# One DMA of 96 partitions for each part of x, a table in parts of 17 and 10 slots, small work on GpSimd, and the first v one step earlier

## The chip, the cores and the metric

The kernel runs on one core of one Trainium2 chip. The metric is the device time of an execution in microseconds.

## The reference

```python
# x: (8, 3072, 256), float32
X = np.fft.fft(np.fft.fft(x, axis=1), axis=2).real      # FNet mixing
x_prev = X shifted by one row along the sequence (zero first)
xk = mu_k * X + (1 - mu_k) * x_prev
xr = mu_r * X + (1 - mu_r) * x_prev
k  = maximum(xk @ w_k, 0)                                # 256 -> 1024
v  = (k * k) @ w_v                                       # 1024 -> 256
out = sigmoid(xr @ w_r) * v                              # (8, 3072, 256), float32
```

## The kernel before

The sequence of 3072 rows is split as 48 x 64. A half of one batch's x lies in a tile `xh` of 96 partitions: partition 48g + n1 holds rows 32g + 16h + (0 to 15) of row block n1. GpSimd issues the loads, which also turn float32 into float16:

```python
x_r = x.rearrange("b (n1 r) d -> b n1 r d", r=R)         # R = 64, N1 = 48, D = 256

def load_part(b, h, n, q0, nq):
    for g in range(2):
        r0 = 32 * g + 16 * h + q0
        nc.gpsimd.dma_start(out=xh_t[b, h][48 * g:48 * g + 48, q0:q0 + nq],
                            in_=x_r[b, :, r0:r0 + nq, :])

def load_xh(b, h):                                       # batches 1 to 7
    xh_t[b, h] = xh_pool.tile([96, 16, 256], FP16, name="xh")    # bufs=2
    load_part(b, h, 1, 0, 16)
```

Per batch, 27 rows of `f` are laid into one partition of `y` by a small DMA, and each pair of finished output tiles is stored by two DMAs of 128 KB from a ring of three buffers. Both are issued by SyncE on one queue, and VectorE waits for them when it reads `y` or reuses `o`:

```python
def flat(b):
    V.memset(y_t[b, "f"][0:1, 0:1], 0.0)
    nc.sync.dma_start(out=y_t[b][0:1, 1], in_=y_t[b, "f"])          # "y<-f"

def v_out(c, tb, n):
    o = o_pool.tile([P, 2, 256], FP32, name="o" ..., bufs=3 if n == 2 else 1)
    V.scalar_tensor_tensor(out=o..., in0=st["v"]..., scalar=16.0, in1=st["r", c]..., ...)
    for s in range(2):
        ...
        eng.dma_start(out=dst, in_=o[64 * s:64 * s + 64, 0:n])      # "out_dram<-o"
```

The rest is one list of 192 steps (one per piece of the k product), to which the other work of this batch and the next is pinned by hand (`v_out` finishes a pair of output tiles); the order on every engine is fixed.

Of the kernel before, what the change touches and what calls it, by code (L numbers as in the profile page):

```python
# [35 lines left out]
def kernel(  # L36
# [18 lines left out]
    NS1 = 9  # L55
# [46 lines left out]
    def load_part(b, h, n, q0, nq):  # L102

        for g in range(2):
            r0 = 32 * g + 16 * h + q0
            nc.gpsimd.dma_start(out=xh_t[b, h][48 * g:48 * g + 48, q0:q0 + nq],  # L106
                                in_=x_r[b, :, r0:r0 + nq, :])

    def load_xh(b, h):
        xh_t[b, h] = xh_pool.tile([96, 16, 256], FP16, name="xh")  # L110
        load_part(b, h, 1, 0, 16)
# [36 lines left out]
    load_part(0, 0, 2, 0, 8)  # L148
# [4 lines left out]
    load_part(0, 0, 2, 8, 8)  # L153
# [5 lines left out]
    load_part(0, 1, 2, 0, 8)  # L159
    load_part(0, 1, 2, 8, 4)  # L160
    load_part(0, 1, 2, 12, 4)
# [136 lines left out]
    def m_rest(part):  # L298



        s = 26 if part else 0
        if part:
            V.tensor_scalar(out=m2[hi64, 25], in0=m1[hi64, 25], scalar1=-1.0, scalar2=None,
                            op0=ALU.mult)
            V.tensor_copy(out=m1[hi64, 25], in_=m1[lo64, 25])
        for n, m in enumerate((m1, m2)):
            V.tensor_scalar(out=m[hi64, s], in0=m[hi64, s], scalar1=-1.0, scalar2=None,
                            op0=ALU.mult)
            if part:  # L310
                V.memset(m[lo64, 25], 0.0)
            else:
                V.tensor_copy(out=mz[lo64, n], in_=m[lo64, 1])
                V.memset(m[:, 0, 0:1], 0.0)
# [11 lines left out]

    g_zeros(13, 24)
# [8 lines left out]
    def loads():  # L336

        V.memset(mu_f, 0.0)
        mus = [mu.rearrange("(a b) -> a b", b=1) for mu in (moe_mu_k, moe_mu_r)]
        for i, mu in enumerate(mus):  # L340
            nc.sync.dma_start(out=mu_f[0:1, 0, i:i + 1], in_=mu[0:1])
            nc.sync.dma_start(out=mu_f[1:65, 0, i:i + 1], in_=mu[1:129:2][0:64])
            nc.sync.dma_start(out=mu_f[65:128, 0, i:i + 1], in_=mu[2:128:2])
        for a in range(2):
            gather(wk_sb[0][a], moe_w_k, a)
        for i, mu in enumerate(mus):
            gather(mu_f[:, 1, i:i + 1], mu, 1)
        load_xh(1, 0)
        for a in range(2):
            gather(wr_sb[0][a], moe_w_r, a)  # L350
        nc.gpsimd.dma_start(out=wv_sb, in_=moe_w_v.rearrange("(fc p) v -> p fc v", p=128))
        load_xh(1, 1)
        for a in range(2):
            gather(wk_sb[1][a], moe_w_k, 2 + a)
        for a in range(2):
            gather(wr_sb[1][a], moe_w_r, 2 + a)
# [12 lines left out]
    def plain_128():  # L369

        V.memset(w_eo[:, 0, 63:64], 1.0)
        V.tensor_scalar(out=w_eo[:, 0, 127:128], in0=w_eo[:, 0, 127:128], scalar1=-2.0,
                        scalar2=1.0, op0=ALU.mult, op1=ALU.add)
        V.memset(u128, 0.0)

        V.tensor_copy(out=tw[lo64, 0, 1:NSL], in_=m1[lo64, 1:NSL, 0])
        V.tensor_copy(out=tw[hi64, 0, 1:NSL], in_=m2[hi64, 1:NSL, 0])
        V.tensor_copy(out=tw[hi64, 1, 1:NSL], in_=m1[hi64, 1:NSL, 0])
        V.tensor_scalar(out=tw[lo64, 1, 1:NSL], in0=m2[lo64, 1:NSL, 0], scalar1=-1.0,
                        scalar2=None, op0=ALU.mult)  # L380
        V.memset(tw[hi64, :, 1:2], 0.0)

        for n, half, sign in ((0, lo64, 1.0), (0, hi64, -1.0), (1, lo64, -1.0), (1, hi64, 1.0)):
            V.tensor_scalar(out=tw[half, n, 0:1], in0=tw[half, n, 2:3], scalar1=sign,
                            scalar2=None, op0=ALU.mult)
# [55 lines left out]
    def d_half(b, u, ps, eng):  # L441
        d_units(b, ps, u, 2)
        evac(g_all[:, u:u + 2, 1:257],
             ps[:, 0:512].rearrange("p (i c) -> p i c", c=256), eng)

# [81 lines left out]
    def mix_short(b, lo, hi):  # L527

        x_t[b, 0, 0] = xo = x_t.get((b, 0, 0)) or mix_pool.tile([P, 2, 1536], FP16, name="x00")
        for a in range(2):  # L530
            V.scalar_tensor_tensor(out=xo[:, a, 64 * lo:64 * hi],
                                   in0=_v(x_t[b], 64 * (26 * a + lo), [(1, 64 * (hi - lo))]),
                                   scalar=mu_f[:, a, 0:1],
                                   in1=_v(y_t[b], 64 * (NSL * a + lo), [(1, 64 * (hi - lo))]),
                                   op0=ALU.mult, op1=ALU.add)
# [4 lines left out]

    def mix2(b, j, m, lo, hi):
        for a in range(2):
            mix(b, j, m, a, lo, hi)
# [41 lines left out]
    def v_tile(c, tb):  # L585

        apart = c == chunks[-1] and tb >= 2
        h = 0 if apart else tb % 2
        if h == 0:
            st["v"] = ps_v()  # L590
        for fc in range(8):
            nc.tensor.matmul(out=st["v"][:, 256 * h:256 * h + 256],  # L592
                             lhsT=k2_t[c][:, fc, 128 * tb:128 * tb + 128],
                             rhs=wv_sb[:, fc], start=(fc == 0), stop=(fc == 7))

    def v_out(c, tb, n):
        b, m, i = c
        o = o_pool.tile([P, 2, 256], FP32, name="o" if n == 2 else f"o{tb}",
                        bufs=3 if n == 2 else 1)
        t0 = tb + 1 - n  # L600

        V.scalar_tensor_tensor(out=o.rearrange("p a b -> p (a b)")[:, 0:256 * n],  # L602
                               in0=st["v"][:, 0:256 * n], scalar=16.0,
                               in1=st["r", c][:, 256 * t0:256 * (t0 + n)],
                               op0=ALU.mult, op1=ALU.mult)
        for s in range(2):
            k = 24 * m + 8 * i + 2 * t0 + s
            dst = dataclasses.replace(out[b, k:k + 1, :], ap=[[48 * D, 64], [2 * D, n], [1, D]])
            eng = nc.scalar if s and n == 1 else nc.sync
            eng.dma_start(out=dst, in_=o[64 * s:64 * s + 64, 0:n])  # L610
# [10 lines left out]
    m_rest(0)  # L621
    loads()
    m_angles(NS1, NSL)
# [8 lines left out]
    m_wrap(NS1, NSL)  # L632
# [7 lines left out]
    d_item(0, 2)  # L640
    m_sine(NS1, NSL)
    d_item(0, 3)
    for lo, hi in ((0, 4), (4, 8)):
        halves(0, lo + (lo > 0), hi + 1)
        diff(0, lo, hi)
        mix_short(0, lo, hi)
# [5 lines left out]
    def at(step, f, *args):  # L652
        work.setdefault((step, "x" if f in (a_item, a_sum, d_item, c_item, r_item) else "w"),
                        []).append((f, args))

    def mirrored_mu():

        for a in range(2):
            V.tensor_copy(out=mu_m[:, a], in_=mu_f[:, 1 - a])
        V.tensor_copy(out=mu_m[0:1], in_=mu_f[0:1])  # L660

    chunks = [(b, m, i) for b in range(B) for m in range(2) for i in range(3)]
    nk = 4 * len(chunks)
    LAG = 5
    keep_busy(4)
    k_products(chunks[0], 0, 0, 256)
    k_products(chunks[0], 1, 0, 256)
    d_half(0, 16, ps_v(), "A")
    d_half(0, 18, ps_v(), "A")
    for n, c in enumerate(chunks):  # L670
        at(4 * n + (5 if n in (0, 2) else 4), r_item, c)


    at(0, m_swap, NS1, NSL)
    at(0, m_rest, 1)
    at(0, mix2, 0, 1, 0, 0, 8)
    at(1, c_item, 0, 9, 8)
    at(1, halves, 0, 9, 17)
    at(1, diff, 0, 8, 16)
    at(1, mix2, 0, 0, 0, 8, 16)  # L680
    at(2, d_item, 0, 5)
    at(2, a_sum, 1, 0, 0)
    at(3, c_item, 0, 17, 8)
    at(5, butterfly, 1, 1, 0)
    at(4, halves, 0, 17, 25)
    at(4, diff, 0, 16, 24)
    at(5, a_sum, 1, 0, 4)
    at(5, a_sum, 1, 0, 8)
    at(5, mix2, 0, 0, 0, 16, 24)
    at(6, a_sum, 1, 0, 12)  # L690
    at(6, c_item, 0, 25, 2)
    at(6, load_xh, 2, 0)
    at(6, mix2, 0, 1, 0, 8, 16)
    at(7, butterfly, 1, 1, 1)
    at(7, halves, 0, 25, 27)
    at(7, diff, 0, 24, 26)
    at(7, mirrored_mu)
    at(7, load_xh, 2, 1)
    at(8, mix, 0, 0, 1, 0)
    at(9, mix, 0, 0, 1, 1)  # L700
    at(10, mix2, 0, 1, 0, 16, 24)
    at(12, mix, 0, 1, 1, 0)
    at(14, mix, 0, 1, 1, 1)
    for n, st0 in enumerate((7, 8, 9, 10)):
        at(st0, a_item, 1, 1, n // 2, n % 2, "A")
    at(5, plain_128)
    for n, st0 in enumerate((12, 13, 13, 14, 15, 17)):
        at(st0, d_item, 1, n)
    at(18, turned, 1)
    for n, st0 in enumerate((14, 15, 18, 19)):  # L710
        at(st0, c_item, 1, (0, 7, 14, 21)[n], 7 if n < 3 else 6)

    for b in range(B):
# [8 lines left out]
        if t < B:  # L722
            for n, st0 in enumerate((9, 10, 12, 14) if b else (11, 13, 15, 24)):
# [9 lines left out]
        if t < B:  # L733
            at(s0 + 16, halves, t, 0, 14)
# [13 lines left out]
    for step in range(nk + LAG):  # L748
# [3 lines left out]
        vs = step - LAG  # L752
        if vs >= 0:
            v_tile(chunks[vs // 4], vs % 4)
        due(step, "w")
        if vs >= nk - 2:
            v_out(chunks[vs // 4], vs % 4, 1)
        elif vs >= 0 and vs % 2:
            v_out(chunks[vs // 4], vs % 4, 2)
# [34 lines left out]
```

## Time and profile before

| | before |
|---|---|
| time, three runs | 458.41 to 458.94 us, median 458.77 |
| profiled execution | 461.26 us, of which 459.5 us are the span of the trace |
| granted TensorE clock | 0.998 |

### The profile page before, as it was taken

The numbers are of one execution on the slowest core, as the hardware profiler recorded it, in microseconds if no ns is written. First come the engines' busy times: TensorE is split into PE (matmuls) and PEld (weight loads), VectorE is DVE, ScalarE is ACT, GpSimd is POOL, SyncE is SP. The second block draws the span as 40 slices with busy tenths as digits, with TensorE's granted clock in tenths as the row PEclk, the third lists the DMA queues.
The fourth block names the chain that finished last, engine by engine and source line by source line (L and its number), as shares of the span: only waits on it lengthen the run. The fifth ranks groups of instructions, "written<-read, shape, count | busy, mean of one in ns | idle before, by whom it ended". The sixth has DMA issues, their size and how long they took to land.

```text
span 459.5 us, 9804 instructions
## 1 busy us (share of the span) xinstructions
PE 447.2 (97%) x4087; PEld 327.6 (71%) x4087; DVE 360.0 (78%) x532; ACT 358.8 (78%) x398; POOL 35.6 (8%) x67
## 2 busy tenths in 40 slices
PE   8879999999999999999999999999999999999996
PEld 4647777777777777777777777777777777676764
DVE  7779988987788877978698777888679855898453
ACT  4689898888877887888887888878887888666661
POOL 8831000000000000000000000000000000000000
PEclk9999999999999999999999999999999999999999
DMA  7894561626622274214722265212222221223223
GB/s 131 128 177 90 120 140 46 124 64 138 124 62 67 49 146 109 70 48 90 164 68 58 59 136 120 69 48 69 55 63 61 56 70 47 71 64 75 70 68 93
DMA packets 32972, 40.25 MB, mean 88 GB/s; under 512 B 4480, under 2 KB 30592, under 8 KB 31584
## 3 DMA queue, kind: packets, MB, share of 16 engines
q1 hardware_dynamic: 28080, 25.07, 21.9%
q0 software_dynamic: 4688, 14.42, 18.8%
q8 instruction: 32, 0.52, 0.5%
q10 hardware_dynamic: 160, 0.13, 0.1%
q14 instruction: 12, 0.10, 0.1%
HBM read 28.84 MB, written 25.17 MB: 118 GB/s over the span
## 4 chain that ended last, share of the span: by engine, by line
PE 93%; ACT 3%; DMA 1%; POOL 1%; issue 1%; DVE 0%; another core or an unknown queue 0%; POOLq 0%
PE psV L592 36%; PE psW L555 35%; PE psW L578 9%; PE psW L431 5%; PE psW L407 4%; PE psW L458 3%; DMA xh<-in_x_dram 1%; ACT rl L565 1%; ACT g_all L395 1%; PE psW L421 1%; POOL xh L106 1%; ACT a L395 0%; ACT L583 0%; ACT pq L395 0%; ACT m L287 0%
## 5 line engine op out<-in xcount | busy, mean ns | idle before, releaser
L565 ACT ACTIVATE rl<-psW 128x1024 f16<-128x1024 f32 x192 | 196.7, 1026 | 80.8 <-PE psW L555 80.4
L555 PE MATMUL psW<-x,wk 128*128 128x512 f16 (+1 forms) x776 | 197.4, 377 | 2.5 <-ACT rl L565 1.5
L592 PE MATMUL psV<-wv_sb,k 128*128 128x256 f16 x1536 | 198.6, 272 | 0.0
L571 DVE TENSOR_TENSOR k<-rl 128x2048 f16<-128x2048 f16 x96 | 117.4, 1224 | 62.5 <-ACT rl L565 61.8
L592 PEld LDWEIGHTS <-k 128*128 128x128 f16 x1536 | 143.7, 98 | 20.3
L555 PEld LDWEIGHTS <-wk 128*128 128x128 f16 x776 | 75.7, 98 | 53.3 <-issue 4.0
L602 DVE SCALAR_TENSOR_TENSOR o<-psV,r 128x512 f32<-128x512 f32 (+1 forms) x97 | 66.3, 684 | 22.9 <-PE psV L592 20.7
L523 DVE TENSOR_TENSOR x<-y,t 128x1536 f16<-128x1536 f16 (+1 forms) x70 | 61.8, 882 | 2.4
L395 ACT ACTIVATE a<-psW 128x768 f16<-128x768 f32 x62 | 49.6, 806 | 4.0 <-PE psW L421 2.1
L578 PE MATMUL psW<-wr,x 128*128 128x256 f16 x384 | 49.8, 273 | 0.0
L583 ACT ACTIVATE r<-psW 128x1024 f16<-128x1024 f32 x48 | 49.0, 1021 | 0.8 <-PE psW L578 0.8
L578 PEld LDWEIGHTS <-x 128*128 128x128 f16 x384 | 37.6, 98 | 14.4 <-issue 0.2
L395 ACT ACTIVATE g_all<-psW 128x1024 f16<-128x1024 f32 (+1 forms) x46 | 46.9, 1022 | 1.1 <-PE psW L431 1.1
L106 POOL DMA_DIRECT2D xh<-in_x_dram x38 | 19.7, 525 | 238.7 <-DVE eo L119 222.7
L431 PEld LDWEIGHTS <-a 128*128 128x128 f16 x384 | 25.1, 98 | 10.0 <-issue 0.2
L407 PEld LDWEIGHTS <-eo 96*128 96x128 f16 x416 | 23.4, 97 | 11.6
L119 DVE TENSOR_TENSOR eo<-xh 96x2048 f16<-96x2048 f16 x26 | 31.5, 1213 | 0.0
L395 ACT ACTIVATE pq<-psW 128x896 f16<-128x896 f32 (+5 forms) x33 | 28.7, 871 | 1.6 <-PE psW L431 1.1
L431 PE MATMUL psW<-w_eo,a 128*128 128x128 f16 x368 | 27.7, 219 | 0.0
L407 PE MATMUL psW<-w_pm,eo 96*128 96x96 f16 x416 | 26.3, 205 | 0.0
L458 PEld LDWEIGHTS <-g_all 128*128 128x128 f16 x459 | 17.8, 98 | 7.7 <-issue 0.7
L510 DVE TENSOR_SCALAR t<-d,mu_f 128x1536 f16<-128x1536 f16 (+1 forms) x38 | 20.6, 543 | 0.1
(106 smaller groups left out, 158.5 us busy)
## 6 DMA issues: line engine op xcount, KB each, us to landing
out_dram<-o SPq DMA_DIRECT2D x190, 128.0 KB
xh<-in_x_dram POOLq DMA_DIRECT2D x28, 384.0 KB
xh<-in_x_dram POOLq DMA_DIRECT2D x6, 192.0 KB
wv_sb<-in_moe_w_v_dram POOLq DMA_DIRECT2D x1, 512.0 KB
xh<-in_x_dram POOLq DMA_DIRECT2D x4, 96.0 KB
out_dram<-o ACTq DMA_DIRECT2D x2, 64.0 KB
out_dram<-o SPq DMA_DIRECT2D x2, 64.0 KB
y<-f SPq DMA_DIRECT2D x7, 3.4 KB
```

What stands on the lines that cost most here:

```text
L395: nc.scalar.activation(out=out_ap, in_=in_ap, func=AF.Copy)
L407: nc.tensor.matmul(out=ps[:, 128 * i:128 * i + 96], lhsT=eo[:, 8 * j + i, e, :], rhs=w_pm[0:96, 0], start=True, stop=True)
L431: nc.tensor.matmul(out=_v(ps, 256 * i + 64 * (1 - e), [(128, 2), (1, 64)]), lhsT=a_t[b][:, e, 2 * u:2 * u + 2, :], rhs=w_eo[:, e, :], star ...
L458: nc.tensor.matmul(out=ps[:, o + 64 * i:o + 64 * i + 64], lhsT=g_all[:, u, col:col + 128], rhs=m[:, sl] if sl != 1 else mz[:, 0 if m is m1 ...
L523: V.tensor_tensor(out=dst, in0=_v(y_t[b], 64 * (NSL * a + lo + 3 * m), [(1, n)]), in1=_v(x_t["t", a], 64 * lo, [(1, n)]), op=ALU.subtract ...
L555: nc.tensor.matmul(out=st["k", ds][:, 512 * hs + lo:512 * hs + hi], lhsT=wk_sb[m][a][:, 128 * fc:128 * fc + 128], rhs=xk[:, a, 512 * i + l ...
L565: nc.scalar.activation(out=st["rl"][:, 2 * ds:2 * ds + 2], in_=st["k", ds].rearrange("p (f t) -> p f t", f=2), func=AF.Relu, bias=0.0, sca ...
L571: V.tensor_tensor(out=k2_t[c][:, 2 * ds - 2:2 * ds + 2], in0=r, in1=r, op=ALU.mult)
L578: nc.tensor.matmul(out=ps[:, 256 * tb:256 * tb + 256], lhsT=x_t[b, 1, m][:, a, 512 * i + 128 * tb: 512 * i + 128 * tb + 128], rhs=wr_sb[m] ...
L583: nc.scalar.activation(out=st["r", c], in_=ps, func=AF.Sigmoid)
L592: nc.tensor.matmul(out=st["v"][:, 256 * h:256 * h + 256], lhsT=k2_t[c][:, fc, 128 * tb:128 * tb + 128], rhs=wv_sb[:, fc], start=(fc == 0), ...
L602: V.scalar_tensor_tensor(out=o.rearrange("p a b -> p (a b)")[:, 0:256 * n], in0=st["v"][:, 0:256 * n], scalar=16.0, in1=st["r", c][:, 256 ...
```

## The change

Its intent is a shorter head: half as many x issues on GpSimd, a first table part that lets one more c item go in front of the steps, less small work on the full VectorE, and v work where TensorE idles. Cut to its core:

```diff
-    NS1 = 9
+    NS1 = 17
-    def load_part(b, h, n, q0, nq):
-        for g in range(2):
-            r0 = 32 * g + 16 * h + q0
-            nc.gpsimd.dma_start(out=xh_t[b, h][48 * g:48 * g + 48, q0:q0 + nq],
-                                in_=x_r[b, :, r0:r0 + nq, :])
+    def load_part(b, h, q0, nq):
+        src = x_r[b, 0:1, 16 * h + q0:16 * h + q0 + nq, :]
+        nc.gpsimd.dma_start(
+            out=xh_t[b, h][:, q0:q0 + nq],
+            in_=dataclasses.replace(src, ap=[[32 * D, 2], [R * D, N1], [1, nq * D]]))
 # m_last (slots 25, 26), plain_128 (tables of column 128) and mirrored_mu:
-        V.tensor_scalar(...) / V.tensor_copy(...)
+        nc.gpsimd.tensor_scalar(...) / nc.gpsimd.tensor_copy(...)
 # loads(): wv before x(1,0); the five x parts of batch 0 issued before the last three iotas
+    v_steps = {4 * n + tb + (LAG if n else LAG - 1): (c, tb) ...}    # first chunk's v: steps 4 to 7
 # [cut: several a, c and d items of batches 0 and 1 go one to four steps later]
```

The new source has three dimensions: 2 slices (stride 8192), 48 rows (stride 16384), and the contiguous rest.

## The prediction

> **What bounds the kernel now.** I read the page first (busy shares and slices), then busy time by stretch, then the chain of waits, then the timeline of the first 50 us engine by engine. From the page:
>
> ```profile
> PE 447.2 (97%) x4087; PEld 327.6 (71%) x4087; DVE 360.0 (78%) x532; ACT 358.8 (78%) x398; POOL 35.6 (8%) x67
> ...
> PE   8879999999999999999999999999999999999996
> ...
> POOL 8831000000000000000000000000000000000000
> ```
>
> Only the first four slices (11.5 us each) and the last show TensorE below nine tenths; GpSimd (POOL) works in the first three alone. By stretch (width, then busy us of PE, PEld, DVE, ACT, POOL; clock, DMA share, GB/s):
>
> ```profile
> 0.00:10.00 10.00, 8.71 (x47) 4.98 (x48) 7.84 (x41) 4.25 (x6) 8.40 (x27) 1.00 0.76 123
> 10.00:20.00 10.00, 7.45 (x99) 5.87 (x98) 7.57 (x25) 5.85 (x10) 8.31 (x10) 1.00 0.78 118
> 20.00:30.00 10.00, 6.66 (x71) 4.49 (x70) 7.44 (x23) 8.18 (x10) 6.65 (x8) 1.00 1.13 178
> 30.00:40.00 10.00, 9.26 (x95) 6.65 (x93) 9.65 (x27) 9.97 (x12) 0.59 (x2) 1.00 0.47 84
> 40.00:50.00 10.00, 10.00 (x94) 7.23 (x92) 9.79 (x20) 8.49 (x11) 1.51 (x3) 1.00 0.94 174
> ```
>
> From 40 us on TensorE is never idle until the tail. The change removes no matmul, so from there only an earlier start counts. Idle TensorE before 40 us is 40 - 8.71 - 7.45 - 6.66 - 9.26 = 7.92 us, of which 1.18 us lie before the first matmul. The ceiling of any gain is thus about 6.7 us, 1.5%. From the chain of waits (start, us, what):
>
> ```profile
> 4.99 6.68 DMA xh<-in_x_dram
> ...
> 20.29 1.03 ACT g_all L395
> 21.32 1.13 ACT m L287
> 22.46 1.90 ACT g_all L395 x3
> 24.36 0.92 ACT rl L565
> ...
> 33.06 1.98 ACT rl L565 x2
> 35.06 1.28 ACT L583
> 36.35 1.03 ACT r L583
> 37.43 1.02 PE psW L555 x4
> ```
>
> Two limits: until 11.7 us the landing of x, from 20 to 37 us ScalarE (ACT), whose order puts the sine of the table's second part (1.13 us) and the sigmoid's table load (1.28) ahead of what TensorE needs. VectorE (DVE) is full too (9.65 of 10). The small table work there, and the issues of the x loads:
>
> ```profile
> 4.43 3.05 POOL L106 DMA_DIRECT2D xh<-in_x_dram  x6
> 22.57 0.46 DVE L294 TENSOR_SCALAR m<-m 64x1152 f16<-64x1152 f16 x1
> 38.55 0.64 DVE L384 TENSOR_SCALAR tw<-tw 64x1 f16<-64x1 f16 x4
> ```
>
> **What the Trainium skill says.**
> "DMA: Bandwidth & Descriptors", section "Why a DMA increments its semaphore by 16 and not by 1": the number of DMA engines is the largest up to 16 that divides the slowest dimension of both sides, though some direct copies from GpSimd get all 16. The old loads have 48 rows on both sides; the new source is 2 x 48 x 2048 beside a destination of 96 rows, so the rule read strictly would give 2 engines. No run shows yet which holds.
> "Perfetto Trace Analysis", section "DMA Instruction — SWDGE (GPSIMD)": such a record ends when the descriptors are written, not when data lands. The trace agrees: 0.5 us for an issue, 6.68 us in the chain for one landing.
> "SBUF — State Buffer", section "Who interferes with whom": GpSimd shares its port pair with VectorE; two-port VectorE modes and two-input operations contend with it. The trace of before hardly shows it, since GpSimd computes only until 10.6 us.
> "ScalarE: Activation LUTs", section "What ACT_TABLE_LOAD costs": about 1283 ns; the trace has 1.28 us.
>
> **The change part by part.**
>
> *One DMA of 96 partitions.* Ten issues in the head become five. An issue of 48 partitions takes 0.50 to 0.67 us whether it moves 96 or 384 KB; the one of wv with 128 x 8 rows takes 1.00 us. Linear in rows: 0.52 + 48 x (1.00 - 0.52)/(1024 - 48) = 0.54 us for 96 rows. So five issues save about 2.6 us of GpSimd; the index arithmetic that started at 7.56 starts near 5.3, and the weight gathers (the last ended at 27.87) start some 2 to 3 us earlier. For x itself the gain is less: from 4 us on the DMA share is about 1, so only the stretch 2 to 4 us (shares 0.77 and 0.62 by single microseconds) can be filled: 0.6 us. TensorE's start on the second half of x moves from 11.80 to about 11.2.
>
> *Table in 17 and 10 slots.* Before 11.8 us VectorE does more: angles of 1088 instead of 576 columns (by the two rows 0.76 and 1.34 us: 1.28, so +0.52), wrap +0.25, swap +0.30; the second zeroing (0.79) goes later. Net +0.3 us. The sine takes 1.18 instead of 0.78 us and ends near 10.1, the evacuations behind it near 11.5: still in front of x. Free here. Later it saves: second angles 1.34 to 0.8 us, second sine 1.24 to about 0.83 us (on ACT's part of the chain, -0.4), second swap 0.93 to 0.6.
>
> *Small work to GpSimd.* VectorE loses the twelve rows of the tables for column 128 (37.58 to 39.19, 1.6 us), the mirrored weights (0.4), the fix-ups of the last slots (23.55 to 24.71, 1.15): about 3.1 us in a stretch where it is full. GpSimd's own [P,1] operations took 0.19 to 0.40 us; about 21 of them cost it 5 to 6 us after the gathers, near 28 to 36 us. Their results are needed from step 8, near 39 us. Some may hold VectorE up: I allow 0.5 us.
>
> *Order.* The first chunk's v tiles come one step earlier (4 to 7, none in step 8); its r item in fact moves from step 5 to 6, and v_out of its first pair stays in step 6. One item of c moves in front of the steps; one d, four a items of batch 1 move one to four steps back. So the table load and sigmoid no longer stand before the k work of chunk 1, and v fills TensorE earlier.
>
> Walking the three engines through the new order with the durations above (evacuation of 1024 columns 1.02, overlapping 0.1; k piece 0.87; v 0.87; square 1.2):
> - second half of x, evacuations, d halves: the d halves start at 14.9 instead of 15.65;
> - c evacuations end at 18.0 instead of 19.37 (an idle 0.92 us of ACT follows there in before); mixes at 19.4 and 21.1 instead of 20.8 and 22.5;
> - relu of pieces 0 to 3 at 22.9, 23.8, 24.8, 25.8; in before 25.3, 26.2, 29.7, 32.3;
> - squares done 27.85 (before 33.7): TensorE waits 1.4 us for them at step 4; v tile 0 at 27.9 instead of 35.75;
> - sigmoid ends near 35.5, TensorE waits 0.2 us; from step 7 on no wait; first v tile of chunk 1 ends at 42.7, before at 47.1.
> Two a items (0.34 us each) are done by then in before and not in after: 47.1 - 42.7 - 0.7 = 3.7 us earlier.
> VectorE at that point is about 4.5 us ahead of before, so it doesn't take over.
> I cut 3.7 to 2.9 for two things. TensorE's records and ACT's waits disagree in the head of before: the c item's matmuls are recorded as ended at 24.39, yet its evacuation starts at 27.29 after 1.11 idle us, with nothing else named. Such lags (0.92, 1.11, 0.41 us) fall in stretches in which GpSimd issues gathers, and my walk has none. And GpSimd may hold VectorE. So 458.8 - 2.9 = 455.9 us.
>
> **The rivals.**
> (a) The expected one: a head shorter by 2 to 4 us, then the same TensorE-bound stream. For: no idle TensorE from 40 us on, the same matmuls. Against: nothing in the profile. 455 to 457 us.
> (b) The wait is exchanged. In step 4 TensorE waits for squares on VectorE, or the lags return in full beside the gathers, and the gain shrinks to 1 us or less: 457.5 to 459. For: ACT and VectorE are both near full from 30 us. Against: each loses work ahead of the first squares.
> (c) GpSimd becomes the late one: its fix-ups wait for the landing of all gathers, and then block the x loads behind them (first one issued at 39.41 before). Against: batch 2's data is first needed near step 13, over 10 us later. If it fails, +1 to +3 us: 459 to 461.
> (d) The 96-row source is spread on 2 DMA engines. A 393 KB part at 2/16 of the near 190 GB/s seen would take about 16 us; the first half of x then lands near 18 us, and batch 1's loads take 30 us and more. That costs 10 us and more: 468 to 475. For: the strict rule. Against: the exception named beside it, and loads of whole rows of 8 KB whose destination still has 96 rows. I give it 8%.
>
> **Range and chances.** (a) 60%, (b) 25%, (c) 7%, (d) 8%. (a) and (b) together span 453.5 to 458.8; that holds about 8 in 10. Faster by over 2% needs 9.2 us, more than the 6.7 us of idle there are: 1%. Slower by over 2% is only (d): 7%. The rest, 92%, is within 2%.
>
> **What would show it.** Right: the five x issues near 0.55 us each and GpSimd free of them before 5 us; second-half matmuls near 11.2; v of chunk 0 near 28 to 30 us; TensorE idle before 40 us down from 7.9 to about 5 us, and the same busy stream behind. Step by step it is wrong if x lands as late as 11.8 (DMA was the limit all along), if ACT idles as long before the c item's evacuation (lags), if VectorE rows beside GpSimd's are longer than before (port), if TensorE has new gaps after 40 us. The whole is wrong if the DMA share in the first 12 us drops to a few tenths.

## More of the kernel before

The profiled execution was 2.5 us longer than the median of the timed ones. Four more lines of its page, to be compared later: packets, MB and engine share of the GpSimd queue; the shares of the chain that ended last; the issues of x (count, then busy us and mean ns of one issue); and the x loads' size.

```profile
q0 software_dynamic: 4688, 14.42, 18.8%
...
PE 93%; ACT 3%; DMA 1%; POOL 1%; issue 1%; DVE 0%; another core or an unknown queue 0%; POOLq 0%
...
L106 POOL DMA_DIRECT2D xh<-in_x_dram x38 | 19.7, 525 | 238.7 <-DVE eo L119 222.7
...
xh<-in_x_dram POOLq DMA_DIRECT2D x28, 384.0 KB
```

TensorE (PE) is the chain; DMA is 1% of it.

## The result, and the profile after

| | before | after |
|---|---|---|
| median, four runs each | 458.59 us | 616.31 us |
| range | 457.86 to 458.94 | 612.74 to 620.32 |
| ratio | | 1.344 (95%: 1.336 to 1.353) |
| granted clock, profiled run | 0.998 | 0.881 |

The result is correct, and a third slower. Ratios here are the mean time of one kernel's runs over that of the other's of the same rounds, so not quite the ratio of the medians. The page after, with the lines that answer to those of before:

```profile
PE   2680790390896946997699947998289999999997
...
PEclk7695796596797967999799976999769999999999
...
q0 software_dynamic: 17152, 14.47, 13.3%
...
PE 49%; DMA 39%; DVE 8%; issue 2%; ACT 1%; SPq 0%; POOL 0%; DVEq 0%; POOLq 0%
...
L105 POOL DMA_DIRECT2D xh<-in_x_dram x19 | 14.2, 752 | 329.4 <-DVE eo L119 263.0
...
xh<-in_x_dram POOLq DMA_DIRECT2D x14, 768.0 KB, 34.6
```

TensorE has holes not only in the first slices but all along, up to slice 29 of 40 (15.5 us each): until about 450 us. DMA has gone from 1% to 39% of the chain. One load of 768 KB takes 34.6 us from issue to landing, and one issue 752 ns. The same data (14.4 MB at the destination) need 17152 packets in place of 4688; in the packet records of the traces all those added are of 4 bytes. The DMA engines' share is *lower* than before, 13.3% of a longer span, and in engine time it is nearly the same: 13.3% of 16 x 618.5 us is 1316 us, 18.8% of 16 x 459.5 us was 1382. So the DMA engines as a whole are not full, and have no more to do; the transfers are slow for another reason. By stretch (columns as in the prediction):

```profile
0.00:10.00 10.00, 4.05 (x11) 1.38 (x11) 8.07 (x40) 1.53 (x2) 8.26 (x23) 0.88 0.43 49
10.00:20.00 10.00, 0.41 (x3) 0.40 (x4) 0.14 (x2) 0.00 (x0) 2.28 (x3) 0.50 0.77 139
20.00:30.00 10.00, 9.38 (x76) 7.73 (x75) 4.82 (x17) 6.62 (x9) 3.38 (x4) 0.76 0.18 25
...
50.00:60.00 10.00, 0.00 (x0) 0.00 (x0) 1.42 (x3) 0.00 (x0) 0.00 (x0) 0.50 0.26 54
...
500.00:560.00 60.00, 60.00 (x540) 44.08 (x539) 44.45 (x58) 47.99 (x53) 0.00 (x0) 1.00 0.26 63
```

Two readings. From 50 to 60 us next to nothing works but two loads of x, issued at 29.5 and 32.9 us; the first lands at 65.6 us: the DMA share is 0.26, and 0.26 x 16 engines = 4.2 busy engines, two for each load. And from 500 us on, when the last load, issued at 414.8 us, has long landed, TensorE is full at clock 1.00. The two stretches in which TensorE stands still show a clock of 0.50, and the busy one after the first, from 20 to 30 us, 0.76. So part of the loss is work done slowly after a hole: the same 4087 matmuls keep TensorE busy for 474.3 us in place of 447.2. Which transfers the chain waits for, in order of time (start, us, what; the rest of the chain is left out):

```profile
1.39 18.16 DMA xh<-in_x_dram
...
30.64 35.34 DMA wr<-in_moe_w_r_dram,row_i
...
78.70 35.83 DMA xh<-in_x_dram
...
133.52 20.64 DMA y<-f
...
167.78 22.48 DMA out_dram<-o
...
276.41 24.79 DMA out_dram<-o
```

Only three of these are the loads' own landings or a gather beside them. The others are the stores and the small spill of f: transfers that the change did not touch. (In the page's shares of the whole chain, the spill has 14%, the stores 11%, the loads 9%, the gather 6%.) The store of 276.41 lands at 301.20; the load of x that was issued at 266.17 lands at 300.79. The other stores agree, as far as the trace shows their landing: the ten after 450 us, when no load is left, take 2.4 to 3.7 us, the eight issued while a load had some 3 us or more to go 4.1 to 24.8. The engines' waits (us in total, times, longest):

```profile
DVE o L604 <- DMA out_dram<-o: 56.1, 10, 9.0
...
DVE d L501 <- DMA y<-f: 48.7, 4, 17.3
...
PE psV L594 <- DVE o L604: 48.0, 9, 12.8
```

In before the wait for the spill is 0.4 us, and there is none for stores.

My first theory (S): the source's slowest dimension is 2, so each load runs on two DMA engines, and everything else that has to pass those engines is held up until the load is through. The packet records of after bear out the holding up. The two stores issued at 275.8 and 276.4 have 256 packets of 1 KB; 196 go in the two microseconds from 277, and from 279 to 285 us the stores' queue gets only 2 to 6 a microsecond through, beside 8 KB packets of the loads that take 0.62 us each. The quarter left over is what 4 of 16 engines would hold. The rival (R): the rest of the change makes the waits. A second rival (Q): one DMA of 96 partitions is slow as such.

### The profile page after: what moved, and what is told of

The parts are those of the page before. It is cut to its first block, busy times and chain, and to the rows that moved or that the text cites. A ratio compares the mean times of both kernels' runs of the same rounds, so it can differ in the third digit from the quotient of the medians.

```text
span 618.5 us, 9765 instructions
## 1 busy us (share of the span) xinstructions
PE 474.3 (77%) x4087; PEld 338.6 (55%) x4087; DVE 356.4 (58%) x501; ACT 359.7 (58%) x398; POOL 36.9 (6%) x69
## 3 DMA queue, kind: packets, MB, share of 16 engines
q0 software_dynamic: 17152, 14.47, 13.3%
## 4 chain that ended last, share of the span: by engine, by line
PE 49%; DMA 39%; DVE 8%; issue 2%; ACT 1%; SPq 0%; POOL 0%; DVEq 0%; POOLq 0%
PE psV L594 19%; PE psW L557 18%; DMA y<-f 14%; DMA out_dram<-o 11%; DMA xh<-in_x_dram 9%; PE psW L580 6%; DMA wr<-in_moe_w_r_dram,row_i 6%; PE psW L430 2%; DVE k L573 2%; DVE x L526 2%; PE psW L461 1%; DVE o L604 1%; PE psW L406 1%; DVE t L513 1%; PE psW L420 1%
## 5 line engine op out<-in xcount | busy, mean ns | idle before, releaser
L594 PE MATMUL psV<-wv_sb,k 128*128 128x256 f16 x1536 | 208.8, 281 | 53.3 <-DVE o L604 48.0
L557 PE MATMUL psW<-x,wk 128*128 128x512 f16 (+1 forms) x776 | 205.7, 388 | 26.0 <-DVE x L526 25.1
L594 PEld LDWEIGHTS <-k 128*128 128x128 f16 x1536 | 147.5, 100 | 80.1 <-issue 48.9
L604 DVE SCALAR_TENSOR_TENSOR o<-psV,r 128x512 f32<-128x512 f32 (+1 forms) x97 | 66.3, 684 | 107.3 <-DMA out_dram<-o 56.1
L557 PEld LDWEIGHTS <-wk 128*128 128x128 f16 x776 | 77.1, 100 | 81.6 <-issue 32.9
L580 PE MATMUL psW<-wr,x 128*128 128x256 f16 x384 | 55.5, 292 | 44.3 <-DVE x L526 24.6
L580 PEld LDWEIGHTS <-x 128*128 128x128 f16 x384 | 39.9, 104 | 63.1 <-DVE x L526 24.9
L526 DVE TENSOR_TENSOR x<-y,t 128x1536 f16<-128x1536 f16 x60 | 57.5, 959 | 2.1
L501 DVE TENSOR_TENSOR d<-y 128x1664 f16<-128x1664 f16 (+3 forms) x19 | 16.8, 885 | 48.9 <-DMA y<-f 48.7
L105 POOL DMA_DIRECT2D xh<-in_x_dram x19 | 14.2, 752 | 329.4 <-DVE eo L119 263.0
## 6 DMA issues: line engine op xcount, KB each, us to landing
xh<-in_x_dram POOLq DMA_DIRECT2D x14, 768.0 KB, 34.6
xh<-in_x_dram POOLq DMA_DIRECT2D x3, 384.0 KB, 18.2
```

Of the source, the lines that this page charges most:

```text
L526: V.tensor_tensor(out=dst, in0=_v(y_t[b], 64 * (NSL * a + lo + 3 * m), [(1, n)]), in1=_v(x_t["t", a], 64 * lo, [(1, n)]), op=ALU.subtract ...
L557: nc.tensor.matmul(out=st["k", ds][:, 512 * hs + lo:512 * hs + hi], lhsT=wk_sb[m][a][:, 128 * fc:128 * fc + 128], rhs=xk[:, a, 512 * i + l ...
L580: nc.tensor.matmul(out=ps[:, 256 * tb:256 * tb + 256], lhsT=x_t[b, 1, m][:, a, 512 * i + 128 * tb: 512 * i + 128 * tb + 128], rhs=wr_sb[m] ...
L594: nc.tensor.matmul(out=st["v", tb - h][:, 256 * h:256 * h + 256], lhsT=k2_t[c][:, fc, 128 * tb:128 * tb + 128], rhs=wv_sb[:, fc], start=(f ...
L604: V.scalar_tensor_tensor(out=o.rearrange("p a b -> p (a b)")[:, 0:256 * n], in0=st["v", t0][:, 0:256 * n], scalar=16.0, in1=st["r", c][:, ...
```

## The experiments

Eighteen runs were made. Unless said otherwise the results are correct. In the diffs "after" is the changed kernel. Times are medians; "before" is the kernel before in the same rounds.

| run | time, us | before, us | ratio (95%) |
|---|---|---|---|
| e1_two_loads | 459.63 | 458.04 | 1.003 (1.002 to 1.005) |
| e2_one_load_only | 615.53 | 458.04 | 1.343 (1.341 to 1.346) |
| e3_row_pairs | 457.24 | 458.04 | 0.998 (0.997 to 1.000) |
| e4_head_only | 473.26 | 458.04 | 1.033 (1.031 to 1.034) |
| e5_slowest4 | 515.86 | 458.33 | 1.125 (1.123 to 1.127) |
| e5_slowest8 | 461.97 | 458.33 | 1.009 (1.007 to 1.010) |
| e6_more_o | 603.50 | 458.33 | 1.314 (1.309 to 1.320) |
| e7_four_pieces | 491.99 | 458.33 | 1.073 (1.071 to 1.075) |
| g2_no_f | 583.45 | 460.02 | 1.267 (1.263 to 1.271) |
| g1_no_f_o6 | 526.39 | 460.02 | 1.144 (1.139 to 1.149) |
| b0_before_again | 458.06 | 458.17 | 1.000 (0.998 to 1.001) |
| f1_small_on_vector | 458.72 | 458.17 | 1.001 (1.000 to 1.003) |
| f2_before_pairs | 456.63 | 458.17 | 0.997 (0.995 to 0.998) |
| f3_lag_back | 457.31 | 458.17 | 1.000 (0.997 to 1.002) |
| f4_mu_on_vector | 462.80 | 460.02 | 1.005 (1.002 to 1.008) |
| f6_table17 | 459.60 | 460.02 | 1.000 (0.998 to 1.002) |
| f4b_mu_on_vector | 456.52 | 457.77 | 0.997 (0.996 to 0.998) |
| e3b_row_pairs | 457.60 | 457.77 | 0.999 (0.998 to 1.000) |

### Is it the loads?

**e1_two_loads**: after, with the old loads.

```diff
-        src = x_r[b, 0:1, ...]; nc.gpsimd.dma_start(out=xh_t[b, h][:, ...], in_=replace(src, ap=[...]))
+        for g in range(2):  # two DMAs of 48 partitions, as before
```

> The kernel after, with only its x loads put back to two DMAs of 48 partitions each; everything else of the change stays. Theory S (the shape of the 96-partition source, two slices of 48 rows, spreads each load over two DMA engines, and that alone makes the slowdown): 454.5 to 457.5 us, a little under the kernel before, clock near 1.0, x loads landing within 2 to 5 us of their issue. Rival R (the rest of the change, above all small table work on GpSimd or the first chunk's v one step earlier, makes a new wait that repeats): 480 us or more, with GpSimd or v_out waits of tens of us.

Measured: 459.63 us, clock 0.998. The big loss is gone, so R falls as its explanation. But the time is above the range that S gave: without its loads the change is 1.6 us *slower* than before. That is a second thing to explain.

**e2_one_load_only**: before, with only the loads of the change.

```diff
-        for g in range(2): ...   # two DMAs of 48
+        in_=dataclasses.replace(src, ap=[[32 * D, 2], [R * D, N1], [1, nq * D]])
```

> The kernel before, with only its x loads changed to one DMA of 96 partitions as in the change. Theory S: 605 to 630 us, with loads of 768 KB taking some 34 us each. Rival R: under 480 us, since then most of the 158 us come from the rest of the change or from its meeting with the loads.

Measured: 615.53 us, clock 0.889, as S said; that is 157 us more than before in the same rounds. This one line is the whole loss.

**e3_row_pairs**: after, still one DMA of 96 partitions, in another order. Row block n1 and half g go to partition 2*n1 + g. Since 2 x 8192 = 16384, the two strides of the source become one: 96 rows at an even stride of 8192, a plain 2-dimensional source with 96 as its slowest dimension. The one table laid along these partitions follows:

```diff
-            in_=dataclasses.replace(src, ap=[[32 * D, 2], [R * D, N1], [1, nq * D]]))
+            in_=dataclasses.replace(src, ap=[[R * D, N1], [32 * D, 2], [1, nq * D]]))
-    V.tensor_scalar(out=hi48, in0=pcol_f, scalar1=48.0, scalar2=None, op0=ALU.is_ge)
+    V.tensor_scalar(out=hi_i, in0=pcol_i, scalar1=1, scalar2=None, op0=ALU.bitwise_and)
+    V.tensor_copy(out=hi48, in_=hi_i)
-    n1f = hi48 * -48.0 + pcol_f;  u48 = k1c_f * n1f * (1.0 / N1)
+    n1f = hi48 *  -1.0 + pcol_f;  u48 = k1c_f * n1f * (0.5 / N1)
```

> The kernel after, one DMA of 96 partitions kept, but with the partitions in another order (row block n1 and half g at partition 2*n1+g), which makes the source one even stride of 8192 elements with 96 rows as its slowest dimension; the table that is laid along these partitions is reordered with it, so the result stays right. Theory S: 454 to 457.5 us, loads of 768 KB landing in 3 to 5 us, since 96 rows divide over 16 engines. Rival Q (one DMA of 96 partitions is slow as such, for its size, its number of descriptors or its single issue): loads still 30 us and more, and 600 us or more in all.

Measured: 457.24 us. From its page:

```profile
q0 software_dynamic: 4384, 14.42, 18.2%
...
L105 POOL DMA_DIRECT2D xh<-in_x_dram x19 | 10.1, 537 | 225.6 <-DVE eo L119 224.5
...
xh<-in_x_dram POOLq DMA_DIRECT2D x14, 768.0 KB, 6.8
```

The same bytes in as many issues land in 6.8 us in place of 34.6 us (more than the 3 to 5 us I expected), an issue takes 537 ns in place of 752, and the extra packets are gone. Q falls: it is not the 96 partitions but the order of the source's dimensions.

**e5_slowest4 and e5_slowest8**: after, with the source as 4 slices of 24 rows, or 8 of 12. They read other rows, so the results are wrong; partitions, bytes and data packets (1344 of 8 KB in the loads of 768 KB) stay.

```diff
-            ap=[[32 * D, 2], [R * D, N1], [1, nq * D]]
+            ap=[[32 * D, 4], [R * D, 24], [1, nq * D]]       # e5_slowest4
+            ap=[[32 * D, 8], [R * D, 12], [1, nq * D]]       # e5_slowest8
```

> The kernel after, with the source of each x load laid out as 4 slices of 24 rows in place of 2 slices of 48 (it reads other rows, so its result is wrong on purpose; rows, bytes and packets are the same). Theory S (as many engines as the largest divisor, up to 16, of the source's slowest dimension): loads of 768 KB take half of 34.6 us, 16.5 to 18.5 us; the whole falls by more than half of its excess, since what holds up stores and spills ends before the buffers run dry: 465 to 510 us. Rival Q (a DMA of 96 partitions in three dimensions is slow for another reason than the number of slices): loads over 30 us, over 590 us.

> As before it with 8 slices of 12 rows (result wrong on purpose). Theory S: loads of 8.5 to 10 us where nothing else is under way, 457 to 462 us. Rival Q: over 590 us.

Measured, first with 4 slices, then with 8:

```profile
xh<-in_x_dram POOLq DMA_DIRECT2D x14, 768.0 KB, 18.8
```

```profile
xh<-in_x_dram POOLq DMA_DIRECT2D x14, 768.0 KB, 11.4
```

With 2, 4, 8 slices and 96 even rows a load takes 34.6, 18.8, 11.4, 6.8 us, and the time in excess of the kernel before is 158, 58, 3.6 and -0.8 us. The load's time nearly halves with each doubling of the slices, as S says, though the last two are longer than the 8.7 and 4.3 us that 34.6 divided by 4 and 8 gives. A constant of 3 us and 63 us divided by 2, 4, 8 and 16 engines give 34.5, 18.8, 10.9 and 6.9 us (an estimate, fitted to these four figures; what the constant is, no run shows). Three forecasts missed: 515.86 us lies 6 us above its range, the landings of 18.8 and 11.4 us lie above 16.5 to 18.5 and 8.5 to 10; 461.97 us is just inside. The excess falls faster than the load's time. That it vanishes once a load ends before buffers run dry is my reading, not shown by itself.

One thing did not stay, though my expectation says so: the packets of 4 bytes, 13248, 5952 and 2304 with 2, 4 and 8 slices, 480 in e3. So these runs leave open whether those packets make the load slow. The packet records settle it: in after they take 8 ns each, 106 us of engine time in all, where the 8 KB packets take 870; and e7 below has 42144 of them while the same half of x lands in less than half the time. The records also show the engines at work. One load of after has two 8 KB packets under way at a time, two loads have four; with 4 slices it is mostly four or eight, with 8 slices eight, and 16 in e3 as in before.

### Head or steady state?

**e4_head_only**: after, the 96-partition load for batch 0 only.

```diff
+        if b == 0:
             nc.gpsimd.dma_start(...)      # 2 x 48, as in after
+        else:
+            for g in range(2): ...        # two DMAs of 48
```

> The kernel after, with the 96-partition load only for the five parts of batch 0; the loads of batches 1 to 7 are two DMAs of 48. Theory S with my second reading (the loss recurs in every batch, since stores, spills and weight gathers share the clogged engines): 470 to 485 us, that is, 15 to 30 us of the 158 us come from the head, and no store or spill takes over 5 us after 60 us. Rival H (the start is what is late, and the rest is a chain of delays and a low clock that follow from it): 560 us or more.

Measured: 473.26 us, inside S's range. (Stores took up to 6.7 us after 60 us, above the 5 that I had named, but in e3 they take up to 6.6.) By stretch, head and steady state:

```profile
10.00:20.00 10.00, 0.00 (x0) 0.00 (x0) 0.19 (x2) 0.00 (x0) 2.35 (x3) 0.50 0.76 140
...
100.00:200.00 100.00, 100.00 (x941) 73.82 (x940) 80.50 (x102) 82.26 (x92) 4.11 (x8) 1.00 0.44 96
```

Against e1 (459.63 us) the slow head costs 13.6 us, and nothing follows from it: from 100 us on TensorE is full. The other 616.31 - 473.26 = 143 us come from the loads of batches 1 to 7.

### How do the loads of later batches cost 143 us?

**e6_more_o**: after, six output buffers.

```diff
-                        bufs=3 if n == 2 else 1)
+                        bufs=6 if n == 2 else 1)
```

> The kernel after, with six output buffers in place of three. Theory V (the steady loss comes mostly through output stores that share the clogged engines: VectorE waits 56 us for output buffers, PE 48 us for VectorE's read of psV): 500 to 570 us, waits of VectorE for output stores under 15 us. Rival T (the loads themselves, or the spill of f and the weight gathers, set the pace, and the stores only fill the time): 595 us or more.

Measured: 603.50 us, outside V's range, inside T's, and with V's waits gone: there is no wait of VectorE for stores left among the listed ones. The time went into another wait instead:

```profile
DVE d L501 <- DMA y<-f: 80.0, 4, 22.6
```

The spill of f, 48.7 us in after, is now 80.0 us. It is issued on the same queue as the stores, and T had named it. Theory V as I had put it (mostly stores) fell; the new one (V2) was that stores and spill are both held up by the loads, so that taking away one lets the time reappear in the other.

**g2_no_f and g1_no_f_o6**: after without the spill's DMA (zeros are written in its place, so the result is wrong), with three and with six output buffers.

```diff
-        nc.sync.dma_start(out=y_t[b][0:1, 1], in_=y_t[b, "f"])
+        V.memset(y_t[b][0:1, 1], 0.0)
-                        bufs=3 if n == 2 else 1)      # g1_no_f_o6 only
+                        bufs=6 if n == 2 else 1)
```

> The kernel after with the one DMA of each batch that lays the 27 rows of f into one partition of y taken out, and zeros written there by VectorE in its place (result wrong on purpose). Theory V2 (spill and stores share clogged engines, and each is part of the loss): 540 to 590 us, the wait for output stores as large as before or larger. Rival T (the loads set the pace, and waits only fill the time): over 600 us.

> The same, and six output buffers in place of three. Theory V2: with both ways closed most of the steady loss is gone and the head, the weight gathers and the loads of batches 1 and 2 are left: 480 to 545 us. Rival T: over 590 us.

Measured: 583.45 and 526.39 us, both inside the ranges of V2. In g2_no_f the wait for stores has grown from 56.1 us:

```profile
DVE o L604 <- DMA out_dram<-o: 69.2, 12, 8.0
```

By ratio, six buffers alone take 0.030 of the time of before off, no spill alone 0.077, both together 0.200: nearly twice their sum. That is the mark of two waits behind one cause, each ready to take the other's place. What the chain of g1_no_f_o6 still waits for are landings of x (18.6, 35.7 and 34.2 us) and of a weight gather (34.3 us), which more output buffers cannot hide.

**e7_four_pieces**: after, each half of x from batch 1 on as four DMAs of 192 KB, each still of 2 slices.

```diff
-        load_part(b, h, 0, 16)
+        for q in range(0, 16, 4):
+            load_part(b, h, q, 4)
```

> The kernel after, with each half of x from batch 1 on loaded by four DMAs of 4 slots (192 KB) in place of one of 16, each still of 2 slices of 48 rows. The two loads of a batch overlapped with each other and took 34 us each, so I think that each DMA takes another pair of engines. Theory P (so it is): four pieces on four pairs, landing 9 to 12 us after their issue, and 470 to 490 us in all, of which most is the head. Rival O (all pieces go over one pair, or over one after the other): the last piece lands 30 us or more after the first one's issue, and 570 us or more.

Measured: 491.99 us, 2 us above the range of P; the pieces landed 13.4 us after their issue in the median (9 to 12 expected). The four of a half were in flight together, and the last landed some 16 us after the first one's issue, where one pair of engines needs 34.6 us for the same bytes. So different DMAs do go over different engines, and the load's pieces spread: the packet records mostly show 6 to 9 of their data packets under way, where one load of after has two. It is the dearer cure: 61 issues of x at 758 ns each, and a head that stays slow.

### Why does the rest of the change not gain?

e1 (two DMAs) and e3 (one good DMA) show that without the bad shape the change is worth +1.6 and -0.8 us, where I had predicted -2.9. As a clock for these small differences I use the end of the n-th relu of the k products on ScalarE (192 in all), taken from the traces in us:

```
relu            before   before again   f2     e3     f4b
4th             32.29    28.44          27.51  25.03  25.01
10th            47.12    44.29          42.58  40.70  40.69
13th            53.02    50.38          48.47  49.38  47.88
21st            73.78    71.15          69.23  70.48  68.99
192nd (last)   449.98   447.34         445.43 446.68 445.19
```

**b0_before_again**: the kernel before, unchanged, for a second profile.

> The kernel before, unchanged, for a second profile. Its first profile is of an execution of 461.26 us, 2.5 us longer than the median of its timed runs, so the idle time that my prediction counted in it may be partly that one execution's. Theory N (it was): this profile's span is 456 to 457 us, idle PE time before 40 us is 4 to 5 us and not 6.7, and the fourth relu of the first chunk ends near 30 us and not at 32.3. Rival M (profiling always costs this kernel those 2.5 us): span 459 to 460 us again.

Measured: span 456.8 us, and two stretches of it:

```profile
10.00:20.00 10.00, 8.21 (x102) 6.10 (x101) 8.63 (x28) 7.28 (x12) 8.30 (x10) 1.00 0.80 125
20.00:30.00 10.00, 8.97 (x103) 6.01 (x102) 9.45 (x25) 9.87 (x13) 6.55 (x8) 1.00 1.10 179
```

In the first profile TensorE was busy 7.45 and 6.66 us there. Idle time before 40 us is 40 - 7.59 - 8.21 - 8.97 - 9.29 = 5.94 us, of which 1.2 before the first matmul, so the ceiling of a gain was about 4.8 us and not 6.7 (my 4 to 5 us hold only without that start). The lags that I had found odd in the head (ScalarE idle after matmuls recorded as ended) were that one execution's. What makes some executions do this stays open.

**f2_before_pairs**: before, with only the loads of e3.

```diff
-        for g in range(2): ...   # two DMAs of 48
+        one DMA of 96, ap=[[R * D, N1], [32 * D, 2], [1, nq * D]], table reordered as in e3
```

> The kernel before with only its x loads changed, to one DMA of 96 partitions in the order of row pairs; no other part of the change. Theory L (one issue in place of two is worth 2.4 us here as well, as between the two forms of the kernel after, 459.63 and 457.24): 455 to 456.5 us. Rival W (in the kernel before another wait, the table or the weights, ends last, and the issues gain nothing): 457.3 to 458.5 us.

Measured: 456.63 us, 1.5 us less than before, 0.1 us above L's range and well below W's. By the medians this one part, done well, gives more than the whole change with the same loads (e3), but the two intervals overlap, so that is not shown.

**f1_small_on_vector**: e3, small work back on VectorE.

```diff
-        nc.gpsimd.tensor_scalar / tensor_copy / memset   # m_last, plain_128, mirrored_mu
+        V.tensor_scalar / tensor_copy / memset
```

> The kernel of row pairs (457.24 us), with the three pieces of small table work that the change moved to GpSimd (last two slots, the row and column table of 128, the mirrored mu) back on VectorE, at the same steps. Theory G (GpSimd's 10.4 us for them come too late: they hold mu_m, and with it the scaling on VectorE for 1.9 us, and PE for 1.3 us after 45 us): 455.5 to 456.8 us, no PE gap of over 1 us between 44 and 50 us. Rival D (VectorE is as full there, and the work costs it as much as the wait did): 457 to 459 us.

Measured: 458.72 us, so D holds and G falls: taking the work from VectorE is worth 1.5 us against e3's 457.24 in other rounds, 1.3 by ratio. Yet in e3 it makes a wait. GpSimd from 36 us on, with VectorE beside it (start, us, engine, line; the timeline of e3):

```profile
36.45 1.21 DVE L119 TENSOR_TENSOR eo<-xh 96x2048 f16<-96x2048 f16 x1
36.54 1.17 POOL L376 TENSOR_SCALAR w_eo<-w_eo 128x1 f16<-128x1 f16 x1
...
37.92 3.22 POOL L381 TENSOR_SCALAR tw<-m 64x26 f16<-64x26 f16 x4
38.23 1.22 DVE L575 TENSOR_TENSOR k<-rl 128x2048 f16<-128x2048 f16 x1
```

An operation on one element per partition takes GpSimd 1.17 us, and ends with VectorE's operation beside it. Four like it on 64 partitions, from 41.36 us on, when VectorE is idle, take 1.05 us together. The whole of the moved work takes from 32.76 to 43.15 us, 10.4 us. The mirrored mu is at its end, and VectorE waits for it; TensorE then has a hole:

```profile
DVE t L515 <- POOL mu_m L661: 1.9, 1, 1.9
```

```profile
45.00:50.00 5.00, 3.67 (x34) 2.51 (x31) 4.97 (x7) 3.16 (x4) 0.00 (x0) 1.00 0.92 188
```

e1 has the same wait of 1.9 us, and TensorE is busy for 3.67 us in the same stretch.

**f4_mu_on_vector**, and again as **f4b_mu_on_vector** beside **e3b_row_pairs**: e3, with only the three copies of mirrored mu back on VectorE.

```diff
-            nc.gpsimd.tensor_copy(out=mu_m[:, a], in_=mu_f[:, 1 - a])
-        nc.gpsimd.tensor_copy(out=mu_m[0:1], in_=mu_f[0:1])
+            V.tensor_copy(out=mu_m[:, a], in_=mu_f[:, 1 - a])
+        V.tensor_copy(out=mu_m[0:1], in_=mu_f[0:1])
```

> The kernel of row pairs (457.24 us), with only the three copies of the mirrored mu back on VectorE, the rest of the small table work left on GpSimd. Theory G2 (VectorE's wait of 1.9 us for these copies, which stand behind 10 us of other work in GpSimd's queue, makes the PE gap of 1.3 us): 455.8 to 456.7 us, the gap gone. Rival D2 (what VectorE does at these steps is too much with or without the wait, as when all small work was on it): 457.0 to 458.5 us, a gap of 1 us as before.

> The kernel of row pairs with the three copies of the mirrored mu on VectorE, again. In its first trace the gap was gone (PE busy 4.93 us between 45 and 50 us, 3.67 us without the edit) and the stretch from the sixth to the seventeenth relu took 1.5 us less. Theory G2: 0.8 to 1.6 us less than the kernel of row pairs in the same rounds, at a clock of 0.998 or more. Rival D2: within 0.4 us of it, or above.

> The kernel of row pairs again, to be compared with the run before it. By its first run 0.998 of the kernel before (1 us less); by either theory the same here.

The first try was inconclusive: on that chip the clock fell to 0.50 between 15 and 20 us in its profiled run and five of its six runs were longer than 462 us, one, at full clock, 459.96. On the next chip, in the same rounds: 456.52 against 457.60 us, 1.1 us less, as G2 said. The stretch of f4b:

```profile
45.00:50.00 5.00, 5.00 (x49) 3.77 (x47) 4.97 (x7) 4.29 (x6) 0.64 (x2) 1.00 0.87 157
```

The hole is gone. The size of the gain is less sure than the hole: the eleven times of e3 and e3b fall into two groups, six near 457.1 and five near 458.0, and both profiles are of the slower one. Against the faster group f4b gains 0.6 us. (One execution of the kernel before on that chip took 2675 us; it is not among the fast runs.)

**f3_lag_back**: e3, the first chunk's v back at steps 5 to 8.

```diff
-               (LAG if n else LAG - 1)
+               LAG
```

> The kernel of row pairs (457.24 us), with the first chunk's v back at a lag of five steps (steps 5 to 8). Theory E (the earlier v fills PE time that is idle around 28 to 36 us): 458 us or more. Rival F (PE is not idle for want of v there, or loses as much where the step 8 is empty): 456.5 to 457.6 us.

Measured: 457.31 us in the median, 0.07 us from e3 (one run of six took 460.6 us). F holds: the earlier v gains nothing.

**f6_table17**: f2, with only the table split of the change.

```diff
-    NS1 = 9
+    NS1 = 17
```

> The kernel before with row pairs (456.63 us), with only the first part of the table grown from 9 to 17 slots. Theory of my prediction (the split of the table costs nothing): 456.2 to 457.1 us. Rival B (the longer first sine, some 0.5 us more on ScalarE, and its products on VectorE stand ahead of the first spectrum): 457.3 us or more.

Measured: 459.60 us, on the chip where the kernel before took 460.02; by ratio it is level with before (0.998 to 1.002), where f2 on another chip was 0.995 to 0.998. The two intervals just meet, and the chips differ, so whether the split costs anything is left open.

The fastest two are f2_before_pairs and f4b_mu_on_vector, at 0.997 of the kernel before. They were not run in the same rounds, and nothing here tells them apart.

## Why the prediction was wrong

**The step that failed is rival (d)**, twice over: in its chance and in its size. I read the strict rule for the number of engines and set 8% against it, "Against: the exception named beside it". The exception did not apply. With (d) fell a step of the main line, *One DMA of 96 partitions*: it has TensorE start on the second half of x near 11.2 us, where the first three parts of x landed at 19.55, 20.62 and 22.08 us; and "the same busy stream behind", where TensorE had holes until 450 us. As the Trainium skill has it in "DMA: Bandwidth & Descriptors", section "Why a DMA increments its semaphore by 16 and not by 1", the count is the largest up to 16 that divides both slowest dimensions, and a transfer from GpSimd that gets fewer than 16 takes consecutive engines from a cursor that moves on. This agrees with the count and with the moving on: 2 slices, 34.6 us; 4, 18.8 us; 8, 11.4 us; 96, 6.8 us; and four small loads spread where one did not (e7). That the engines are consecutive no run shows.

The sizes in (d) that concern the load itself were right. It said 16 us for a part of 393 KB and a first half landing near 18 us: the parts took 18.2 us, and the first half, two of them, was there at 20.62. It said 30 us and more for batch 1's loads: the first took 36.1, and all of 768 KB 34.6 in the median. And "468 to 475" for the whole is what e4 measures for a slow head alone, 473.26 us; since (d) counted slow loads of batch 1 in, and e4 has none, that match is partly luck. What (d) left out is that the loads come back in every batch, and that other transfers have to pass the engines they fill: 143 of the 158 us come after the head, and some 90 of these go when spill and stores are freed (g1). I counted only the lateness of the data that the load brings, and not that of the stores and the spill beside it. e6, g2 and g1 show it: neither wait alone, but both together are most of it. The other 50 us or so after the head no run splits further. In g1's chain two loads of x and a weight gather stand for 35.7, 34.2 and 34.3 us, so that the data of the early batches comes late too is the likely rest.

**What bounds the kernel, and the ceiling.** TensorE-bound from 40 us on was right for the kernel before, and e1 and e3 agree. The ceiling of 6.7 us was read from an execution 2.5 us longer than the timed ones; the second profile gives 4.8 us.

**The walk, term by term**, read from e3, the change as it was meant (-0.8 us in its first rounds, -0.2 in the second, where -2.9 was predicted):

- *x issues.* 0.54 us for 96 rows was right for an even stride (537 ns) and wrong for the shape in the diff (752 ns). Alone the good load is worth 1.5 us (f2).
- *Small work.* VectorE's relief was worth 1.3 to 1.5 us (f1). But GpSimd needed 10.4 us for it, not 5 to 6, likely since its operations wait for VectorE's large ones beside it. I had read of that in the Trainium skill, "SBUF — State Buffer", section "Who interferes with whom" (a VectorE operation with two inputs in SBUF contends with a GpSimd operation that reads SBUF). e3's timeline agrees for one operation: 1.17 us for a column of one element, ending 0.05 us after VectorE's operation, where four such took 1.05 us beside an idle VectorE. I had given it no number. My "I allow 0.5 us" for holding VectorE up measured 0.6 to 1.1 us (f4b). That is rival (c) in another form: mu came late, not the x load.
- *v one step earlier.* Worth nothing (f3).
- *The lead in steps.* I took the lead at the first v tile of chunk 1 as the gain, less 0.7 us for two postponed a items. e3 leads the second profile of before by 44.29 - 40.70 = 3.6 us at the tenth relu, but only by 0.67 us at the twenty-first and at the end. With the hole removed (f4b) it leads by 3.6, then 2.2 us. So the deduction for work that was only moved later was too small: what f4b gives back is 1.4 us, where I took off 0.7.
- *The table* was called free; f6 doesn't settle it.
- *Two slips.* The span 453.5 to 458.8 for (a) and (b) together isn't that of their ranges, 455 to 459. And the evacuation at 27.29 us did not wait with "nothing else named": the chain has TensorE's matmuls of L431, to 27.27 us, before it.

**The sign that I named.** "The whole is wrong if the DMA share in the first 12 us drops to a few tenths": it is 0.43 in the first 10 us, 0.76 before (0.47 and 0.78 in the first 12).

## What to carry to other kernels

When two DMAs become one, look at the slowest dimension of both sides as the instruction carries it, and order the partitions so that strides merge into one even stride. A slow load is not only late itself: ask which stores and small copies have to pass the same DMA engines, and what waits for those. Profile the kernel before twice before its idle time is taken as the ceiling of a gain, and count work that a schedule moves later before a lead in steps is called a gain.

## What the Trainium skill lacked or had wrong

- "DMA: Bandwidth & Descriptors": the exception that gives some direct copies from GpSimd all 16 engines isn't told by shape. A source of [2, 48, 4096] against 96 partitions did not get it (34.6 us for 768 KB, two packets under way at a time), nor did [4, 24] (18.8 us) or [8, 12] (11.4 us). All these loads convert float32 to float16; whether that keeps them from the exception, no run here shows.
- The same page: it tells that all transfers share the 16 engines, but not what a load on few of them costs the others. Here stores and a 3.4 KB spill, which are on another queue, waited up to 25 us beside it. Freed from both waits the kernel ran 90 us faster, where the late loads of the head cost 13.6 us.
- The same page: the issue's cost by shape. 96 rows took GpSimd 537 ns with an even stride, 752 ns as 2 x 48, and 601 ns as 8 x 12; and the GpSimd queue had 17152 packets in place of 4384, all of the difference of 4 bytes.
